# Seeds of an S4 convolution kernel without square roots: arc tangent of a turned ratio, modulus by its sine and cosine, and another prologue order

## The chip, the cores and the metric

One core of a Trainium2 chip runs the whole program. The metric is the device time of one launch in microseconds (us). Engines are called as in the profile: PE is TensorE (matmuls), DVE is VectorE, ACT is ScalarE, POOL is GpSimd, SP is SyncE, which here only issues DMAs.

## What is computed

A conditioned block. Six modulation rows come from one vector, a state space layer is applied as a long convolution, and a bilinear gated unit follows. Sizes: L = 2048 positions, D = 640 channels, N = 192 states, F = 1536.

```python
mod = (silu(c) @ w_mod).reshape(6, D)                 # sa, ca, ga, sb, cb, gb
h = layernorm(x) * (1 + ca) + sa
dt = exp(log_dt)[:, None];  A = A_re + 1j*A_im
P = exp((dt * A)[:, :, None] * arange(L))             # D x N x L
K = einsum("dn,dnl,dn->dl", C, P, dt * B).real        # one filter per channel
y = irfft(rfft(h padded) * rfft(K padded))[:L] + h * Dskip
x = x + ga * y
h = layernorm(x) * (1 + cb) + sb
x = x + gb * (((h @ w_gate) * (h @ w_up)) @ w_down)
```

The filter K is the real part of a sum of 192 terms per channel, each of which is a modulus and a phase: C·B·dt gives the start of both (the weight's modulus, and its angle), dt·A_re gives the step of the modulus' logarithm and dt·A_im the step of the phase.

## The kernel before, in words

The channels are split into five blocks `db` of 128. For each block `u_seeds(db)` (L595) works out small 128x192 tables, the seeds: the logarithm's step `rho`, the phase step `f` in turns, the weight's modulus `amp`, and the weight's angle, which becomes the integer phase `psi`. The seeds are written as steps with one letter each, and the strings `SEG0` (block 0, run in the prologue, loop at L1401) and `SEG` (blocks 1 to 4, dropped into the main loop at times from a table) say which steps run together and in what order:

- l loads; a forms rho and f; b forms x and y, the weight's real and imaginary part (L648 to L651).
- c transposes rho and f on PE (`trans`, L617 to L620, three passes each) and squares x and y on ACT; u adds the squares (L687); d and D build integer phase tables DL and DH for the block's two halves (L667 to L675).
- r and R (L681, L683) build the arguments RL and RH of the exponentials, half by half. e and E take the exponentials on ACT (tables LP, RH, RL).
- x takes the square root on ACT and |x|, and the sign of x on DVE (L693). f (L706 to L711) forms amp, and y/(|x|+modulus), with a reciprocal at L708. g is the arc tangent on ACT, whose half angle is doubled later by a scale.
- G transposes amp, h the angle; v (L736, L737) copies both out of PSUM as RL's fourth row and as psi.

From the seeds POOL builds tables (`tab_ph` L768, `tab_eq` L790, doublings at L766) and then outer products at L802: integer phases Ph, and the moduli EQ and EP, 40 "segments" in all, eight to a block. ACT turns phases into sine and cosine (`trig` L841: ab, tra or trb), DVE multiplies the two (QtA and QtB at L857 to L859, PtA at L864, PtB at L884), and PE sums over the states (kg, L899 and L914). Buffers EQ and EP are two deep, Pha and Phb too. Around these, units of the transforms (multiplications at L1022 to L1028, for example) and of the layer norm (BATCH_NORM_STATS2 at L565, the row statistics' reciprocal square root at L371 to L378) are placed at due times of a written table (`T0`), each engine working through its own instructions in the order in which the program issues them. The order strings of the buffers (`SLOT`) name the ring buffer of each use.

The modulation rows need silu(c), `sil`, which ACT forms in `mod_i`; in the prologue that stands right behind step b (P_MOD = 1). `modrow` (L451, matmul at L455) multiplies `sil` with pieces of w_mod, which `mod_l` (L442) loads into two buffers that later hold other tables, t_tw and t_ti. These matmuls are issued before the first kg matmuls, and the third piece is loaded into t_tw again only once the matmuls on the first piece have read it.

After about 530 us follows the gated unit, bound by its matmuls (L1182 and L1597); no seed work is left there. ACT's functions come in sets: an ACT_TABLE_LOAD stands before an ACTIVATE whose function isn't in the loaded set.

Of the kernel before, what the change touches and what calls it, by code (L numbers as in the profile page):

```python
# [10 lines left out]
F32 = mybir.dt.float32  # L11
# [7 lines left out]
P = 128  # L19
D = 640  # L20
# [294 lines left out]
def tile_kernel(ctx: ExitStack, tc: tile.TileContext, I, out):  # L315
# [268 lines left out]
    LP = [pk1.tile([P, 96, 8], F32, name=f"LP{i}") for i in range(3)]  # L584
    LH = pk1.tile([P, 192, 8], I32, name="LH")
    for t in LP:
        V.memset(t[:, :, 0:1], 1.0)
    RH = [pk1.tile([P, 11, 96], F32, name=f"RH{i}") for i in range(3)]
    RL = [pk1.tile([P, 4, 96], F32, name=f"RL{i}") for i in range(2)]
# [5 lines left out]
    def u_seeds(db):  # L595
# [7 lines left out]
        rho, f, amp = prm[:, 0, :], prm[:, 1, :], prm[:, 0, :]  # L603
        x, u, y, v = tb_[:, 0, :], tb_[:, 1, :], ta[:, 1, :], ta[:, 1, :]
# [3 lines left out]
        Rh, Rl, Dh, Dl, Lp = ([R[(2 * db + h) % len(R)] for h in range(2)] for R in (RH, RL, DH, DL, LP))  # L608
        g4 = lambda t: t.rearrange("p k (s r) -> p k s r", r=24)
# [7 lines left out]
        def trans(src, o):  # L617
            PE.matmul(o[:, :, 0:16], src[:, 0:128], perm[:, 0:128], start=True, stop=True)
            PE.matmul(o[0:64, :, 16:24], src[:, 128:192], perm[:, 128:192], start=True, stop=True)
            PE.matmul(o[64:128, :, 16:24], src[:, 128:192], perm[:, 192:256], start=True, stop=True)  # L620
# [32 lines left out]
        def s_c():  # L653
            ps = bank("ps").rearrange("p c (s r) -> p c s r", r=24)
            T["ps"] = ps
            trans(rho, ps[:, 0])
            trans(f, ps[:, 1])
            q = bank("q")
            act(u, x, AF.Square)
            act(q[:, 0], y, AF.Square)  # L660

        def s_d(h):
            ps, q = T["ps"], T["q"]
            sti = q[:, 1].bitcast(I32).rearrange("p (s r) -> p s r", r=24)
            free(h, "lh", "ph")
            if h == 0:
                V.tensor_copy(sti, ps[:, 1])  # L667
# [6 lines left out]
            if h:  # L674
# [3 lines left out]
        def s_r(h):  # L678
            ps = T["ps"]
            free(h, "ep", "eq", "lq")  # L680
            V.tensor_tensor(g4(Rl[h])[:, 0:3], ps[:, 0, hs[h]].unsqueeze(1).to_broadcast([P, 3, 4, 24]),  # L681
                            mults[:, 11:14].unsqueeze(2).unsqueeze(3).to_broadcast([P, 3, 4, 24]), op=OP.mult)
            V.tensor_tensor(g4(Rh[h]), ps[:, 0, hs[h]].unsqueeze(1).to_broadcast([P, 11, 4, 24]),  # L683
                            mults[:, 0:11].unsqueeze(2).unsqueeze(3).to_broadcast([P, 11, 4, 24]), op=OP.mult)

        def s_u():
            V.tensor_tensor(u, u, T["q"][:, 0], op=OP.add)  # L687
# [7 lines left out]
        def s_e(h):  # L695
            for l in range(1, 8):
                act(Lp[h][:, :, l : l + 1], Rl[h][:, 0].unsqueeze(2), AF.Exp, scale=64.0 * l)
            act(Rh[h], Rh[h], AF.Exp)
            act(Rl[h][:, 0:3], Rl[h][:, 0:3], AF.Exp)
            mark("lp", 2 * db + h)  # L700

        def s_f():
            pe = T["pe"]
            if db:
                need(1, "gg")
            V.scalar_tensor_tensor(amp, u, dt2[:, db : db + 1], pe[:, 1], op0=OP.mult, op1=OP.mult)  # L706
            V.scalar_tensor_tensor(pe[:, 0], pe[:, 0], 1e-37, u, op0=OP.max, op1=OP.add)
            V.reciprocal(pe[:, 0], pe[:, 0])  # L708
            V.scalar_tensor_tensor(y, y, 2.0, pe[:, 1], op0=OP.mult, op1=OP.mult)
            V.tensor_tensor(pe[:, 0], y, pe[:, 0], op=OP.mult)  # L710
            V.tensor_scalar(y, pe[:, 0], 1.0, -1.0, op0=OP.min, op1=OP.max)  # L711

        def s_G():
            if db:
                ps = bank("ps2")
            else:
                ps = ring(ps_tr, [P, 2, 512], "tr")[:, :, :N]
            T["ps2"] = ps.rearrange("p c (s r) -> p c s r", r=24)
            trans(amp, T["ps2"][:, 0])
            if db == 0:  # L720
                for h in range(2):
                    act(g4(Rl[h])[:, 3], T["ps2"][:, 0, hs[h]])

        def s_g():
            if db:
                s_G()
            act(y, y, AF.Arctan)

        def s_h():
            trans(y, T["ps2"][:, 1])  # L730

        def s_v():
            ps = T["ps2"]
            if db:
                for h in range(2):
                    V.tensor_copy(g4(Rl[h])[:, 3], ps[:, 0, hs[h]])  # L736
            V.tensor_scalar(psi, ps[:, 1], 4294967296.0 / math.pi, None, op0=OP.mult)  # L737
# [6 lines left out]
            for h in range(2):  # L744
# [4 lines left out]
        steps = dict(l=s_l, a=s_a, b=s_b, c=s_c, d=one(s_d, 0), D=one(s_d, 1), r=one(s_r, 0), R=one(s_r, 1), u=s_u, x=s_x,  # L749
                     e=one(s_e, 0), E=one(s_e, 1), f=s_f, G=s_G, g=s_g, h=s_h, v=s_v)  # L750
# [39 lines left out]
    def tab_eq(hf):  # L790
# [4 lines left out]
        rl = RL[hf % 2]  # L795
# [22 lines left out]
    def mk_ep(n):  # L818
        hf, s = divmod(n, 4)
        r = slice(s * 24, s * 24 + 24)  # L820
        need(1, "lp", hf)
        mark("ep", n)
        outer(EP[n % 2], LP[hf % 3][:, r], RH[hf % 3][:, 3::-1, r], 24, 4, OP.mult)

    def mk_eq(n):
# [4 lines left out]
        outer(EQ[n % 2], LQ[:, r], RH[hf % 3][:, 3:11, r], 24, 8, OP.mult)  # L830
# [566 lines left out]
    SY.dma_start(dcol, I["A_Dskip"].rearrange("(b p) -> p b", p=P))  # L1397
    exp_acc(dt, ldt)
    V.tensor_scalar(dt2, dt, 2.0, None, op0=OP.mult)
    due(-101)  # L1400
    for i, _ in enumerate(gp0):  # L1401
        due(i - 100)
        if i == P_PH:
            tab_ph(0, 1)
            mk_ph(0, 1)
        elif i == P_EP:
            mk_ep(0)
        elif i == P_MOD:
            mod_i()
    tab_eq(0)  # L1410
    tab_ph(0, 0)
    mk_ph(0, 0)
    mk_eq(0)
# [350 lines left out]
```

## Time and profile before

| what | value |
| --- | --- |
| time, median of 3 runs | 995.83 us (995.24 to 996.85) |
| the profiled execution's own time | 1000.16 us |
| its span in the trace | 998.3 us |
| granted clock of PE, mean | 0.955 |
| PE busy | 889.1 us (89%) |
| DVE busy | 770.0 us (77%) |
| ACT busy | 581.0 us (58%) |
| POOL busy | 574.7 us (58%) |

The busy shares are averages over stages of different kind. The prologue (to about 27 us) makes block 0's seeds, the main loop (to about 430 us) works through the 40 segments, and the rest is the last transforms and the gated unit. A row of the timeline is the start, the duration, the engine, the line and the operation, with what came out and went in; in square brackets stands how long the engine had been idle before and what released it. A row of a table by stretches gives the busy time of each engine with its instructions. A row of the chain gives start, duration and what the program's end was waiting for at that time.

### The profile page before, as it was taken

What the parts mean: (1) busy time and instruction counts of PE and PEld (TensorE: products, weight loads), DVE (VectorE), ACT (ScalarE), POOL (GpSimd) and SP (SyncE); (2) the same over time, 40 slices, a digit from 0 to 9 for tenths busy, and PEclk for the clock granted to TensorE, in tenths of its full rate; (3) what the DMA queues carried; (4) which work ended last, traced back from release to release, by engine and by line L of the source; (5) the groups of instructions that cost most, each with busy time, mean ns of one, the idle gap of its engine ahead of it and who ended that gap; (6) DMA issues with size and microseconds to landing.
All of it is one profiled execution on the core that took longest, in us unless ns stands there. A gap on an engine that the chain in (4) does not pass through costs nothing.

```text
span 998.3 us, 26784 instructions
## 1 busy us (share of the span) xinstructions
PE 889.1 (89%) x11190; PEld 728.2 (73%) x11190; DVE 770.0 (77%) x1391; ACT 581.0 (58%) x1055; POOL 574.7 (58%) x424
## 2 busy tenths in 40 slices
PE   4874699799889778997988999999999999999998
PEld 3653466576666466776766888879998888889998
DVE  8698568987989988795989877787576887768452
ACT  4759999987889797874574222235473422224331
POOL 4976899899869989960056667650112454442000
PEclk9867799899989989999999999999999999999999
DMA  7654665454545534559732542535635232212341
GB/s 243 239 145 155 217 237 163 159 165 135 154 131 161 171 108 149 161 152 305 221 113 59 188 169 69 184 132 159 211 133 202 96 98 80 79 53 63 96 159 53
DMA packets 141961, 148.96 MB, mean 149 GB/s; under 512 B 8976, under 2 KB 120080, under 8 KB 140432
## 3 DMA queue, kind: packets, MB, share of 16 engines
q1 hardware_dynamic: 140688, 146.33, 46.3%
q8 instruction: 88, 1.44, 0.6%
q10 hardware_dynamic: 1152, 0.92, 0.3%
q14 instruction: 33, 0.27, 0.1%
HBM read 108.36 MB, written 38.86 MB: 147 GB/s over the span
## 4 chain that ended last, share of the span: by engine, by line
PE 59%; ACT 14%; DVE 13%; issue 6%; POOL 5%; DMA 2%; DVEq 0%; SPq 0%; ACTq 0%; POOLq 0%
PE pa L1182 26%; PE pa L1597 16%; ACT tra L320 2%; ACT L320 2%; PE psfc L981 1%; ACT trb L320 1%; PE kg L899 1%; PE psfb L981 1%; PE psfa L1041 1%; PE kg L914 1%; POOL EQ L802 1%; PE psfb L1041 1%; PE psfa L981 1%; PE psfc L936 1%; POOL Pha L802 1%
## 5 line engine op out<-in xcount | busy, mean ns | idle before, releaser
L802 POOL TENSOR_TENSOR EQ<-LQ,RH 128x1536 f32<-128x1536 f32 x40 | 124.2, 3105 | 21.9 <-DVE QtB L859 21.7
L320 ACT ACTIVATE z<-pa 128x512 f32<-128x512 f32 x24 | 14.4, 599 | 166.4 <-PE pa L1182 115.4
L1146 DVE TENSOR_TENSOR wsgl<-wga,wsgh 128x640 fp32r<-128x640 f32 x72 | 68.2, 950 | 46.7 <-ACT wsgh L320 46.7
L320 ACT ACTIVATE wsgh<-wga 128x640 fp32r<-128x640 f32 x72 | 52.6, 732 | 71.2 <-PE pa L1597 39.8
L1546 POOL TENSOR_TENSOR z<-z,s 128x512 f32<-128x512 f32 x24 | 33.5, 1395 | 98.6 <-DVE s L1545 98.6
L1597 PE MATMUL pa<-wsgh,sh 128*128 128x384 f32 (+1 forms) x304 | 69.6, 310 | 0.0
L1597 PE MATMUL pa<-wsgl,sh 128*128 128x384 f32 (+1 forms) x304 | 69.3, 309 | 0.0
L1597 PE MATMUL pa<-wsgh,sl 128*128 128x384 f32 (+1 forms) x304 | 69.2, 309 | 0.0
L802 POOL TENSOR_TENSOR EP<-LP,RH 128x768 f32<-128x768 f32 x40 | 66.1, 1653 | 0.0
L1158 POOL TENSOR_TENSOR tf<-wur,wgb 128x256 f32<-128x256 f32 x24 | 19.2, 801 | 80.9 <-DVE wtl L1146 54.7
L802 POOL TENSOR_TENSOR Pha<-LH,DH 128x1536 int32<-128x1536 int32 (+1 forms) x21 | 62.5, 2974 | 3.0 <-ACT trb L320 2.6
L802 POOL TENSOR_TENSOR Phb<-LH,DH 128x1536 int32<-128x1536 int32 x20 | 62.3, 3117 | 2.9 <-ACT tra L320 2.9
L1146 DVE TENSOR_TENSOR wtl<-tf,wth 128x256 fp32r<-128x256 f32 (+1 forms) x72 | 60.0, 859 | 0.0
L914 PE MATMUL kg<-QtB,PtB 64*32 64x64 f32 x2560 | 47.9, 226 | 8.4 <-DVE QtB L858 8.4
L914 PEld LDWEIGHTS kg<-QtB,PtB 64*32 64x32 f32 x2560 | 40.9, 113 | 16.0 <-DVE QtB L858 9.5
L1544 DVE TENSOR_TENSOR s<-pa,s 128x512 f32<-128x512 f32 x24 | 16.6, 691 | 45.2 <-PE pa L1182 40.1
L1182 PE MATMUL pa<-sl,wth 128*128 128x512 f32 x144 | 45.2, 395 | 2.1 <-DVE sl L1146 2.1
L1597 PEld LDWEIGHTS pa<-wsgh,sl 128*128 128x128 f32 x304 | 46.6, 188 | 0.0
L1597 PEld LDWEIGHTS pa<-wsgl,sh 128*128 128x128 f32 x304 | 46.6, 188 | 0.0
L1597 PEld LDWEIGHTS pa<-wsgh,sh 128*128 128x128 f32 x304 | 46.5, 188 | 0.0
L1182 PE MATMUL pa<-sh,wth 128*128 128x512 f32 x144 | 45.1, 395 | 1.1 <-ACT sh L320 1.1
L1182 PE MATMUL pa<-sh,wtl 128*128 128x512 f32 x144 | 45.4, 397 | 0.0
(608 smaller groups left out, 2957.3 us busy)
## 6 DMA issues: line engine op xcount, KB each, us to landing
wga<-wdg SPq DMA_DIRECT2D x24, 640.0 KB, 4.0
wga<-B_w_gate SPq DMA_DIRECT2D x12, 640.0 KB, 5.7
wgb<-B_w_gate SPq DMA_DIRECT2D x24, 320.0 KB, 3.4
wur<-B_w_up SPq DMA_DIRECT2D x24, 320.0 KB, 4.0
xb<-x2d SPq DMA_DIRECT2D x6, 1280.0 KB, 7.4
TVb<-WD SPq DMA_DIRECT2D x22, 256.0 KB, 3.4
t_tw<-w_mod SPq DMA_DIRECT2D x3, 1600.0 KB, 7.8
t_ti<-w_mod SPq DMA_DIRECT2D x3, 1600.0 KB, 7.7
```

The source lines that it names most:

```text
L320: return S.activation(o, i, f, **kw)
L802: G.tensor_tensor(o.rearrange("p x (h l) -> p x h l", l=8), lo.unsqueeze(2).to_broadcast([P, rows, nh, 8]), hi.rearrange("p h x -> p x h") ...
L899: PE.matmul(kg[j * 32 : j * 32 + 32, dd, :], PtA[:, c, dl * 4 + j, :], QtA[:, c, dl * 4 + j, :], start=dd == 0 and c == 0, stop=False, til ...
L914: PE.matmul(kg[j * 32 : j * 32 + 32, dd, :], PtB[lo : lo + 64, c, r, :], QtB[lo : lo + 64, c, r, :], start=False, stop=dd == 7 and c == 1, ...
L981: PE.matmul(r[c][par * 64 : par * 64 + 64, i, :], t_tw[:, k0 + k, c, :], src[:, k, :], start=True, stop=True, tile_position=(0, par * 64))
L1041: PE.matmul(r[par][:, i], w, v, start=c == 0, stop=c == 1, tile_position=(lo, 0))
L1146: V.tensor_tensor(lo, v, hi, op=OP.subtract)
L1158: G.tensor_tensor(t[:, 0:2], u[:, 0:2], g[:, 0:2], op=OP.subtract)
L1182: PE.matmul(ps, w[a][:, k], x[b][:, l], start=n == 0 and m == 0, stop=n == 2 and m == len(ks) - 1)
L1544: V.tensor_tensor(S67[i], ps, S6[i], op=OP.add)
L1546: G.tensor_tensor(ZT[i], ZT[i], S67[i], op=OP.add)
L1597: PE.matmul(ACC[tb][t][c], x[:, ts], w[:, cs], start=st, stop=f == NF - 1 and n == 2 and (c == 0 or t % 2 == 1))
```

## The change

1. No square root, square or absolute value. Step x (now L700 to L704) forms a sign from x·y, sgn = ±0.5, and turns (x, y) by an eighth of a circle toward the axis, so that the ratio y/x lies within ±1; step X (L708 to L711) forms that ratio with a reciprocal. ACT takes its arc tangent, and then the sine and the cosine of the angle. The modulus is x·cos + y·sin: step m (L725) scales both products, and `trans` (L625) sums the two in PSUM while it transposes them, six passes where amp took three. Step n (L720) adds the turn of a quarter circle times sgn back to the angle.
2. For blocks 1 to 4 the exponentials of both halves are taken together (B, E): LP, RH and RL are single tiles, and one instruction takes both halves where two stood.
3. The prologue has another order. A first sine of a constant stands ahead of everything on ACT, `mod_i` (silu) moves from behind step b to behind steps m and G, where mk_ep, tab_eq and mk_eq stand as well, and tab_ph(0,0) with mk_ph(0,0) stands behind steps v and r, ahead of the exponentials' outer products.

ACT_TABLE_LOADs in the program: 24 before, 16 after.

```diff
-SEG0 = ("l", "a", "b", "c", "ud", "r", "x", "e", "f", "G", "g", "D", "h", "v", "R", "")
-SEG = ("l", "a", "b", "c", "ud", "D", "r", "R", "x", "eE", "f", "g", "h", "v")
-P_PH, P_EP, P_MOD = 3, 6, 1
+SEG0 = ("l", "a", "b", "cx", "d", "X", "f", "nh", "vr", "e", "mG", "D", "", "", "R", "")
+SEG = ("l", "a", "b", "cx", "d", "D", "X", "B", "f", "E", "nm", "G", "h", "v")
+P_PH, P_PSI, P_EP = 3, 7, 9
...
-            q = bank("q")
-            act(u, x, AF.Square)
-            act(q[:, 0], y, AF.Square)
+            bank("q")
...
-        def s_u():
-            V.tensor_tensor(u, u, T["q"][:, 0], op=OP.add)
...
         def s_x():
-            pe = bank("pe")
-            act(u, u, AF.Sqrt)
-            act(pe[:, 0], x, AF.Abs)
-            V.tensor_scalar(pe[:, 1], x, 0.0, 0.5, op0=OP.is_ge, op1=OP.subtract)
+            q = T["q"][:, 0]
+            V.tensor_tensor(q, x, y, op=OP.mult)
+            V.tensor_scalar(sgn, q, 0.0, 0.5, op0=OP.is_ge, op1=OP.subtract)
+            V.scalar_tensor_tensor(prm, tb_[:, 1::-1, :], 2.0, sgn.unsqueeze(1).to_broadcast([P, 2, N]), op0=OP.mult, op1=OP.mult)
+            V.tensor_tensor(x, x, prm[:, 0, :], op=OP.add)
+            V.tensor_tensor(y, y, prm[:, 1, :], op=OP.subtract)
+
+        def s_X():
+            q = T["q"][:, 0]
+            V.reciprocal(q, x)
+            V.tensor_scalar(q, q, 3e38, -3e38, op0=OP.min, op1=OP.max)
+            V.tensor_tensor(q, y, q, op=OP.mult)
+            V.tensor_scalar(arg, q, 1.0, -1.0, op0=OP.min, op1=OP.max)
 
         def s_f():
-            pe = T["pe"]
+            T["pe"] = pe = bank("pe")
+            act(arg, arg, AF.Arctan)
+            act(pe[:, 1], arg, AF.Sin)
+            act(pe[:, 0], arg, AF.Sin, scale=-1.0, bias=halfpi)
+
+        def s_n():
+            V.scalar_tensor_tensor(arg, sgn, 0.5 * math.pi, arg, op0=OP.mult, op1=OP.add)
+
+        def s_m():
             if db:
                 need(1, "gg")
-            V.scalar_tensor_tensor(amp, u, dt2[:, db : db + 1], pe[:, 1], op0=OP.mult, op1=OP.mult)
-            V.scalar_tensor_tensor(pe[:, 0], pe[:, 0], 1e-37, u, op0=OP.max, op1=OP.add)
-            V.reciprocal(pe[:, 0], pe[:, 0])
-            V.scalar_tensor_tensor(y, y, 2.0, pe[:, 1], op0=OP.mult, op1=OP.mult)
-            V.tensor_tensor(pe[:, 0], y, pe[:, 0], op=OP.mult)
-            V.tensor_scalar(y, pe[:, 0], 1.0, -1.0, op0=OP.min, op1=OP.max)
+            V.scalar_tensor_tensor(xy, xy, dt2[:, db : db + 1], T["pe"], op0=OP.mult, op1=OP.mult)
+
+        def s_e(*hh):
+            lp, rh, rl = (halves(R, hh) for R in (LP, RH, RL))
+            for l in range(1, 8):
+                act(lp[:, :, :, l], rl[:, :, 0], AF.Exp, scale=64.0 * l)
+            act(rh, rh, AF.Exp)
+            act(rl[:, :, 0:3], rl[:, :, 0:3], AF.Exp)
...
         def s_G():
...
-            trans(amp, T["ps2"][:, 0])
+            ps = p2()
+            trans(ps[:, 0], x, y)
...
-        def s_g():
-            if db:
-                s_G()
-            act(y, y, AF.Arctan)
...
+    act(colT[:, 0:1], halfpi, AF.Sin)
     exp_acc(dt, ldt)
-    V.tensor_scalar(dt2, dt, 2.0, None, op0=OP.mult)
+    V.tensor_scalar(dt2, dt, math.sqrt(0.5), None, op0=OP.mult)
...
+        elif i == P_PSI:
+            tab_ph(0, 0)
+            mk_ph(0, 0)
         elif i == P_EP:
+            mod_i()
             mk_ep(0)
-        elif i == P_MOD:
-            mod_i()
-    tab_eq(0)
-    tab_ph(0, 0)
-    mk_ph(0, 0)
-    mk_eq(0)
+            tab_eq(0)
+            mk_eq(0)
```

Three places show what the change does to the engines' orders. In the names, tra and trb are the PSUM buffers of sine and cosine, which also serve block 0's transposes; psfa to psfc are a ring of PSUM banks; ptb, pta and prm are the seeds' tiles in SBUF (ptb holds x and y); ct holds the permutation for the transposes; ccol is c.

ACT from its first instruction on, before: silu is the fourth ACTIVATE.

```order
L320 ACT_TABLE_LOAD
L320 ACTIVATE prm<-pta,dt 128x192
L320 ACTIVATE psfb<-ptb 128x2x192
L320 ACT_TABLE_LOAD
L320 ACTIVATE sil<-ccol 128x5
L320 ACTIVATE ptb<-ptb 128x192
L320 ACTIVATE psfa<-pta 128x192
L320 ACT_TABLE_LOAD
```

The same place after; the two rows of psfb<-pta are the sine and the cosine.

```order
L320 ACTIVATE psfb<-ptb 128x2x192
L320 ACTIVATE pta<-pta 128x192
L320 ACTIVATE psfb<-pta 128x192
L320 ACTIVATE psfb<-pta,halfpi 128x192
L320 ACT_TABLE_LOAD
L320 ACTIVATE LP<-RL 128x96 x7
L320 ACTIVATE RH<-RH 128x1056
L320 ACTIVATE RL<-RL 128x288
L320 ACTIVATE RL<-tra 128x2x96
L320 ACT_TABLE_LOAD
L320 ACTIVATE sil<-ccol 128x5
L320 ACTIVATE TVb<-psfb 1x256
```

Silu, with a table load of its own ahead of it, now stands behind the arc tangent, the exponentials and the copy of the transposed modulus.

PE from its fifth row on, after: the transposes of the angle (pta) and of x and y (ptb), and then the first modulation row. Before, three passes of amp (prm) stood there ahead of three of the angle, and the same row behind them.

```order
L625 MATMUL tra<-ct,pta 128x8x16
L625 MATMUL tra<-ct,pta 64x8x8 x2
L625 MATMUL tra<-ct,ptb 128x8x16 x2
L625 MATMUL tra<-ct,ptb 64x8x8 x4
L455 MATMUL psfb<-t_tw,sil 128x256 x5
```

The modulation row keeps its place behind the seeds' transposes, whose number grows from six to nine.

DVE in the main loop, where block 2's seeds stand between the products of two segments, before:

```order
L857 TENSOR_TENSOR QtA<-tra,EQ_143 128x32x32
L858 TENSOR_TENSOR QtA<-tra,EQ_143 128x16x32
L859 SCALAR_TENSOR_TENSOR QtA<-tra,EQ_143 128x16x32
L687 TENSOR_TENSOR ptb<-ptb,psfc 128x192
L667 CAST psfc<-psfa 128x192
```

And after:

```order
L869 TENSOR_TENSOR QtA<-tra,EQ_143 128x32x32
L870 TENSOR_TENSOR QtA<-tra,EQ_143 128x16x32
L871 SCALAR_TENSOR_TENSOR QtA<-tra,EQ_143 128x16x32
L700 TENSOR_TENSOR psfc<-ptb 128x192
L701 TENSOR_SCALAR pta<-psfc 128x192
L702 SCALAR_TENSOR_TENSOR prm<-ptb,pta 128x384
L703 TENSOR_TENSOR ptb<-ptb,prm 128x192
L704 TENSOR_TENSOR ptb<-ptb,prm 128x192
L676 CAST psfc<-psfa 128x192
```

One instruction with an operand in PSUM (psfc) gives way to five, and L700, L702, L703 and L704 read two operands from SBUF.

More of the change, by code (lines that the diff above doesn't have):

```diff
@@ L702, in s_f @@
-        def s_f():
-            pe = T["pe"]
+            for h in hh:
+                free(h, "ep", "eq", "lq")
+            w = slice(4 * hh[0], 4 * hh[-1] + 4)
+            for R, n, k in ((RL, 3, 11), (RH, 11, 0)):
+                o = halves(R, hh)[:, :, 0:n]
+                src = ps[:, 0, w].rearrange("p s r -> p (s r)").rearrange("p (h x) -> p h x", h=len(hh))
+                V.tensor_tensor(o, src.unsqueeze(2).to_broadcast([P, len(hh), n, 96]),
+                                mults[:, k : k + n].unsqueeze(1).unsqueeze(3).to_broadcast([P, len(hh), n, 96]), op=OP.mult)
@@ L734, in s_v @@
             if db:
-                for h in range(2):
-                    V.tensor_copy(g4(Rl[h])[:, 3], ps[:, 0, hs[h]])
-            V.tensor_scalar(psi, ps[:, 1], 4294967296.0 / math.pi, None, op0=OP.mult)
+                V.tensor_copy(RL[:, 0:2, 3], ps[:, 0].rearrange("p (h s) r -> p h (s r)", h=2))
+            V.tensor_scalar(psi, ps[:, 1], 2147483648.0 / math.pi, None, op0=OP.mult)
             def weighted(h):
```

74 lines of the change are left out of this document (33 added, 41 removed).

## The prediction

> **What bounds the kernel now.** I read the page's busy shares first, then the busy time by stretches.
>
> ```profile
> PE 889.1 (89%) x11190; PEld 728.2 (73%) x11190; DVE 770.0 (77%) x1391; ACT 581.0 (58%) x1055; POOL 574.7 (58%) x424
> ```
>
> ```profile
> 27.40:80.00 52.60, 36.43 (x571) 28.77 (x569) 44.14 (x95) 34.72 (x63) 42.52 (x25) 0.79 0.61 181
> 80.00:130.00 50.00, 31.77 (x644) 24.40 (x646) 35.38 (x69) 49.47 (x85) 40.63 (x27) 0.74 0.61 205
> 180.00:230.00 50.00, 45.26 (x1014) 35.06 (x1016) 43.35 (x71) 44.42 (x84) 44.70 (x29) 0.93 0.49 153
> 530.00:998.00 468.00, 458.85 (x2422) 404.78 (x2422) 328.57 (x523) 163.57 (x317) 172.64 (x158) 1.00 0.37 121
> ```
>
> The columns are the stretch, its length, and the busy time of PE, PEld, DVE, ACT and POOL. The 89% of PE come from the last stage (458.85 of 468 us), which the change doesn't touch. In the main loop three engines are close together: in 180 to 230 DVE has 43.35, ACT 44.42 and POOL 44.70 us of 50. From 80 to 130 ACT alone is full, 49.47 of 50. So a microsecond of ACT is worth one in block 1, and in blocks 2 to 4 DVE and ACT count about alike. Then I read the chain of what ended last, at the prologue:
>
> ```profile
> 17.15 0.37 ACT pta L320
> 17.56 0.79 PE tra L618 x2
> ...
> 18.77 4.57 PE psfb L455 x10
> ...
> 27.05 6.77 DMA t_tw<-w_mod
> ...
> 39.57 1.03 PE kg L899 x64
> ```
>
> The program's end hangs on the first modulation row. It starts at 18.77; once the matmuls of this piece have read t_tw, another piece of w_mod is loaded there; and behind the matmuls on that load stands the first kg at 39.57. What starts this row later moves the whole chain.
>
> **The prologue: +7.7 us.** The prices of its steps are in these rows of the timeline:
>
> ```profile
> 8.79 0.34 DVE L651 TENSOR_TENSOR pta<-pta,psfb 128x192 f32<-128x192 f32 x1
> ...
> 10.05 0.37 DVE L667 CAST psfa<-psfc 128x192 int32<-128x192 f32 x1
> ...
> 11.80 0.45 DVE L681 TENSOR_TENSOR RL<-psfc,mults 128x288 f32<-128x288 f32 x1
> 12.17 1.25 DVE L683 TENSOR_TENSOR RH<-psfc,mults 128x1056 f32<-128x1056 f32 x1
> ...
> 17.02 0.87 DVE L565 BATCH_NORM_STATS2 st<-f16a 128x6 f32<-128x320 f32 x2
> ```
>
> ```profile
> 8.03 0.21 ACT L320 ACTIVATE sil<-ccol 128x5 f32<-128x5 f32 x1
> ...
> 12.77 1.43 ACT L320 ACTIVATE LP<-RL 128x96 f32<-128x96 f32 x7
> 13.99 1.08 ACT L320 ACTIVATE RH<-RH 128x1056 f32<-128x1056 f32 x1
> ...
> 15.85 1.28 ACT L320 ACT_TABLE_LOAD   x1
> ```
>
> Before, silu was ready at 8.24, so the row waited for nothing but PE. After, silu stands behind the whole seed chain. In order: y ends at 9.13 (L651). Step x is four 128x192 operations at about 0.39 (L651's 0.34 and the gap to the next) and one of 128x384 at 0.56, 2.1. Step d is 1.75 (from 10.05 to 11.80) and 0.27 for t64, 2.0. Step X is a reciprocal of 1.40 (L708 in block 4's rows below, with its gap) and three operations at 0.39, 2.6. Arc tangent, sine and cosine are three times 0.37, as pta at 17.15: 1.1. Step n is 0.4, the angle's transpose 1.2 (from 17.56 to 18.77), psi 0.4, RL and RH 1.6 (11.80 to 13.42). Layer norm statistics come next on DVE, 1.1 (L565 and its aggregate), and m, 0.6. The exponentials run beside these and cost nothing: 2.6 us from RL on end at 22.0, before m at 22.2. The transposes of x and y have six passes each where 1.2 us had three, 2.4; the copy on ACT 0.4, the load 1.28, silu 0.2. The sum is 9.13 + 2.1 + 2.0 + 2.6 + 1.1 + 0.4 + 1.2 + 0.4 + 1.6 + 1.1 + 0.6 + 2.4 + 0.4 + 1.28 + 0.2 = 26.5, against 18.77: **+7.7**. Queued behind the waiting row on PE are five more rows and every kg; SP's reload of t_tw waits for them. The three loads fewer in the prologue lie on ACT before this point and are in the sum. If all of it were swallowed by later idle time, the term would be 0. I take it whole, since each link of the chain releases the next without slack.
>
> The load's price has two readings. The trace has 1.28 us, and the next ACTIVATE starts 0.02 us after its end (15.85 + 1.28 = 17.13, and pta starts at 17.15). The Trainium skill, page "ScalarE: Activation LUTs", section "What ACT_TABLE_LOAD costs", adds a drain of 1.38 us to each, 2.66 us in all. By it the eight loads that go would be worth 21.3 us and by the row 10.3 us; the trace disagrees with the drain, and the sum goes by the row.
>
> **Block 1: −2.4 us.** The loads on ACT from 95 to 110 us, as one group, and POOL's first operation after the place of block 1's step x:
>
> ```profile
> L320 ACT ACT_TABLE_LOAD x4 | 5.1, 1283 | 0.0
> ```
>
> ```profile
> 82.48 3.10 POOL L802 TENSOR_TENSOR EQ<-LQ,RH 128x1536 f32<-128x1536 f32 x1 [7.07 <-DVE QtB L859]
> ```
>
> Two of these loads go (2 × 1.28). The joint exponentials save 0.75: LP's seven stand 0.18 apart for 96 columns (the row at 12.77), one of 192 columns about 0.27, so seven pairs save 0.6, and the pairs of RH and RL the rest. Squares, root and absolute value less two sines are two ACTIVATEs at 0.27, 0.5. Together −3.9, all of it on a full engine. Against it stands DVE's step x of 2.1 us less 0.6 for L687 and its gap, ahead of the row statistics on which ACT's layer norm waits: +1.5. Net **−2.4**. POOL is idle for 7.07 us up to 82.48, so DVE doesn't stall there.
>
> **Blocks 2 to 4 on DVE: +1.25 us each, and stalls.**
>
> ```profile
> 356.22 0.40 DVE L706 SCALAR_TENSOR_TENSOR prm<-ptb,dt,psfc 128x192 f32<-128x192 f32 x1
> ...
> 357.06 1.37 DVE L708 RECIPROCAL psfc<-psfc 128x192 f32<-128x192 f32 x1
> ...
> 359.25 0.36 DVE L711 TENSOR_SCALAR pta<-psfc 128x192 f32<-128x192 f32 x1
> ```
>
> L706 to L711 take 3.4 us (356.22 to 359.61), and L687 and L693 0.55. The joint copies and products save 0.45. Added are x 2.1, X 2.6, n 0.4 and m 0.56, together 5.65: net +1.25. The stalls are the larger part. Two operands in SBUF cost DVE this, while POOL ran its own:
>
> ```profile
> 51.02 0.17 DVE L480 TENSOR_TENSOR mcol<-mcol 128x5 f32<-128x5 f32 x1
> 51.22 1.43 DVE L481 TENSOR_SCALAR mcol<-mcol 128x5 f32<-128x5 f32 x1
> 52.68 3.01 DVE L482 TENSOR_TENSOR mcol<-mcol 128x5 f32<-128x5 f32 x1
> ```
>
> ```profile
> 50.00 2.62 POOL L766 TENSOR_TENSOR LH<-LH,DL 128x384 int32<-128x384 int32 x2
> 52.58 3.09 POOL L802 TENSOR_TENSOR EQ<-LQ,RH 128x1536 f32<-128x1536 f32 x1
> ```
>
> L482 multiplies five columns and takes 3.01 us: it ends at 55.69, where POOL's EQ ends at 55.67. L481 ends with POOL's doubling at 52.62. L480, of the kind that takes 0.17, got through between. So such an operation waits for the end of the running POOL operation, or gets through free: 0 to 3.1 us. The seeds before had an operand in PSUM in each of these operations, and didn't wait. Where x will stand, POOL runs without a gap:
>
> ```profile
> 159.32 0.34 DVE L687 TENSOR_TENSOR ptb<-ptb,psfc 128x192 f32<-128x192 f32 x1
> ...
> 260.50 0.34 DVE L687 TENSOR_TENSOR ptb<-ptb,psfc 128x192 f32<-128x192 f32 x1
> ...
> 343.16 0.34 DVE L687 TENSOR_TENSOR ptb<-ptb,psfc 128x192 f32<-128x192 f32 x1
> ```
>
> ```profile
> 159.17 3.11 POOL L802 TENSOR_TENSOR Pha<-LH,DH 128x1536 int32<-128x1536 int32 x1
> ...
> 162.92 1.52 POOL L766 TENSOR_TENSOR LQ<-LQ,RL 128x192 f32<-128x192 f32 x2
> ...
> 258.15 3.11 POOL L802 TENSOR_TENSOR Pha<-LH,DH 128x1536 int32<-128x1536 int32 x1
> 261.22 3.10 POOL L802 TENSOR_TENSOR EQ<-LQ,RH 128x1536 f32<-128x1536 f32 x1
> ...
> 341.73 3.10 POOL L802 TENSOR_TENSOR EQ<-LQ,RH 128x1536 f32<-128x1536 f32 x1
> 344.79 1.64 POOL L802 TENSOR_TENSOR EP<-LP,RH 128x768 f32<-128x768 f32 x1
> ```
>
> L700 would wait 2.96 (159.32 to 162.28), 0.76 and 1.67 us, mean 1.8. Then L701 reads PSUM, and L702, 0.74 us behind the end of that wait, meets the next operation: 1.4, 2.3 and 0.9 us, mean 1.5. L703 and L704 follow at once, and I take them as free like L480. For n I take half of a 1.64 us EP, 0.8. Together **4.1 us a block**, an estimate within 0 and 10. Queued behind the stalled x on DVE are d and the next segment's QtA and PtA, for which PE's kg and POOL's buffers wait.
>
> No row shows a SCALAR_TENSOR_TENSOR (L702, L720) waiting like this. The Trainium skill, page "SBUF — State Buffer", section "Who interferes with whom", says that any DVE instruction with two SBUF inputs contends with a POOL instruction that reads SBUF, under an exclusive lock; it speaks against this change. By it the 4.1 stands, and if only the kinds seen to wait did so, it would be 1.8; L482's 3.01 agrees.
>
> **Blocks 2 to 4 on ACT: −2.5 us each.** One load (1.28), 0.75 and 0.5, as in block 1. In block 3, POOL's wait for psi shrinks too:
>
> ```profile
> 286.07 0.39 POOL L742 TENSOR_TENSOR DL<-ptb 128x96 int32<-128x96 int32 x1 [8.09 <-issue]
> ```
>
> ```profile
> 283.20 0.35 ACT L320 ACTIVATE pta<-pta 128x192 f32<-128x192 f32 x1
> ```
>
> The arc tangent at 283.20 came behind 6.5 us of exponentials and loads; it will stand ahead of them. Between nothing and 4.6 us of POOL's 8.09 go; I take half, −2.3.
>
> **The sum.** 7.7 − 2.4 + 3 × (1.25 + 4.1 − 2.5) − 2.3 = +11.5. The profiled execution took 1000.16 us (span 998.3), so its like would take 1011.7 us; the median of the runs is 4.3 lower, 995.83 + 11.5 = **1007** us.
>
> **The rivals.** (B) Ports don't stall DVE: the larger operations get through as L480 did. Then 12.3 go, and 995 us is left. For it speaks L480 at 0.17, while POOL's L766 ran; against it, that POOL has no gap at these places and that the two operations behind L480 waited. (C) The other side: ACT alone sets the pace of blocks 2 to 4. DVE's 1.25 + 4.1 = 5.35 us fit into its idle time (50 − 43.35 = 6.65 us in a stretch that holds one block's seeds), and only ACT's relief counts: 7.7 − 2.4 − 7.5 − 2.3 = −4.5, 991 us, faster. It decides once a block's DVE surplus stays below those 6.65 us and falls where nothing waits; against it, POOL waited 7.07 us for DVE's QtB ahead of 82.48. (D) L703 loses as well, as L482 did right behind L481: another 3.1 a block, 1017 us. (E) The late first row is swallowed by idle time further on, such as the 7.07 us ahead of 82.48: 7.7 less, 1000 us.
>
> **How the numbers follow.** Chances: forecast 0.50, B 0.14, C 0.14, D 0.14, E 0.08. A measurement of this kernel can tell about 0.2% (2 us) from no change. B straddles that bound, 0.09 within, 0.03 above and 0.02 below; the forecast's low tail adds 0.01 within; C is faster in 0.13 and within in 0.01. So faster 0.15, same 0.11, slower 0.74. The range leaves out D's upper and C's lower part: 991 to 1020 us.
>
> **What would show it.** The first modulation row should start near 26.5 and the first kg near 47; were it before 42, the prologue is wrong. L700 and L702 should last 1 to 3 us in blocks 2 to 4, ending with POOL operations, and 0.4 and 0.6 in the prologue; were they short everywhere, B holds. ACT in 80 to 130 should still be full. Should L703 be long, D holds. If DVE is long but PE's kg come no later by segment, C holds. The last stage should keep its length of 468 us; if that moved, no part of this would tell why.

## The result, and the profile after

The changed kernel takes 1040.74 us (median of 4 runs) against 995.54 us for the kernel before: the ratio is 1.0438, with a 95% interval of 1.0394 to 1.0481. It is 45 us slower, where I had forecast 11.5 us slower and a range that ended at 1020. The direction was right, and so were the prologue's term and the mechanism of the waits for POOL. A PSUM bank that is held longer was not in the sum at all, and the terms for the work of DVE and ACT were wrong.

The page of the profile after, first part, and below it the busy time by stretches (stretch, its length, then PE, PEld, DVE, ACT, POOL):

```profile
span 1041.4 us, 26793 instructions
...
PE 900.2 (86%) x11220; PEld 734.1 (70%) x11220; DVE 784.2 (75%) x1392; ACT 568.2 (55%) x1001; POOL 575.6 (55%) x424
```

```profile
80.00:130.00 50.00, 28.08 (x541) 20.15 (x544) 37.45 (x82) 40.56 (x64) 35.14 (x25) 0.73 0.55 164
...
180.00:230.00 50.00, 38.61 (x826) 29.87 (x830) 36.88 (x56) 38.32 (x65) 32.49 (x20) 0.85 0.39 120
...
280.00:330.00 50.00, 34.38 (x695) 24.68 (x695) 40.61 (x69) 34.96 (x60) 29.76 (x23) 0.86 0.45 133
...
380.00:430.00 50.00, 30.76 (x704) 22.94 (x706) 41.33 (x70) 33.22 (x55) 34.91 (x24) 0.83 0.29 86
```

The span grew by 43.1 us, and no engine's busy time by more than 14.2. In 180 to 230, which holds most of block 2's seeds, every engine is idle more than before: PE has 38.61 where it had 45.26, DVE 36.88 (43.35), ACT 38.32 (44.42) and POOL 32.49 (44.70). ACT is no longer full in 80 to 130, 40.56 of 50. When all engines lose busy time at once, they are most likely waiting for each other, and the question is where the ring of waits is closed.

To find the place I took the starts of the same 40 POOL operations (EQ at L802, now L814) in both traces and subtracted. The table gives the lag of the n-th EQ in us; the rows left out lie between their neighbours, to within 1 us.

| segment | before, start | after, lag | what lies between |
| --- | --- | --- | --- |
| 3 | 52.58 | 7.0 | the prologue |
| 8 | 121.06 | 9.3 | block 1's seeds |
| 11 | 150.19 | 11.0 | |
| 13 | 172.25 | 11.4 | block 2's seeds begin |
| 15 | 192.46 | 23.9 | |
| 21 | 253.50 | 23.8 | nothing |
| 24 | 296.66 | 31.7 | block 3's seeds |
| 29 | 341.73 | 31.7 | nothing |
| 32 | 376.41 | 43.4 | block 4's seeds |
| 39 | 436.96 | 43.4 | nothing, to the program's end |

The lag comes in steps, one at each block's seeds, and from block 2 on it is neither made nor given back between them. The last stage keeps its 468 us. Blocks 2, 3 and 4 cost 12.9, 7.9 and 11.7 us, where my sum had 2.85 each and 2.3 less in block 3.

**The prologue** went as forecast. Two rows of ACT and two of PE:

```profile
24.40 1.28 ACT L320 ACT_TABLE_LOAD   x1
25.69 0.21 ACT L320 ACTIVATE sil<-ccol 128x5 f32<-128x5 f32 x1
```

```profile
25.95 4.63 PE L455 MATMUL psfb<-t_tw,sil 128*128 128x256 f32 x10 [1.96 <-ACT sil L320]
...
47.09 1.10 PE L911 MATMUL kg<-QtA,PtAa 128*32 128x64 f32 x64
```

The row that started at 18.70 now starts at 25.95 (forecast 26.5), and the first kg at 47.09 (forecast near 47).

**Block 2** shows most of what was missing. First DVE's step x, and the POOL operations beside it:

```profile
171.83 1.65 DVE L700 TENSOR_TENSOR psfc<-ptb 128x192 f32<-128x192 f32 x1
173.51 0.36 DVE L701 TENSOR_SCALAR pta<-psfc 128x192 f32<-128x192 f32 x1
173.98 0.56 DVE L702 SCALAR_TENSOR_TENSOR prm<-ptb,pta 128x384 f32<-128x384 f32 x1
174.57 0.59 DVE L703 TENSOR_TENSOR ptb<-ptb,prm 128x192 f32<-128x192 f32 x1
175.09 1.03 DVE L704 TENSOR_TENSOR ptb<-ptb,prm 128x192 f32<-128x192 f32 x1
...
184.59 0.36 DVE L711 TENSOR_SCALAR pta<-psfc 128x192 f32<-128x192 f32 x1
189.88 1.22 DVE L869 TENSOR_TENSOR QtA<-trb,EQ 128x1024 f32<-128x1024 f32 x1 [4.94 <-ACT tra L320]
```

```profile
170.15 3.11 POOL L814 TENSOR_TENSOR Pha<-LH,DH 128x1536 int32<-128x1536 int32 x1
173.20 0.49 POOL L808 COPY LQ<-RL 128x96 f32<-128x96 f32 x1
```

L700 takes 1.65 us instead of 0.37 and ends at 173.48, just behind POOL's Pha (173.26). L703 and L704 lose 0.2 and 0.7. That is the wait for POOL that I had counted, 2.2 us here. The larger event is on PE, and then on ACT:

```profile
185.00 0.70 PE L993 MATMUL psfc<-ghb,t_tw 128*64 128x128 f32 x4 [7.58 <-DVE pta L711]
185.48 0.64 PE L993 MATMUL psfb<-ghb,t_tw 128*64 128x128 f32 x4
```

```profile
188.30 0.60 ACT L320 ACTIVATE ghb<-psfc 128x512 f32<-128x512 f32 x1 [6.32 <-PE psfc L993]
```

PE was idle for 7.58 us until DVE's L711, the last operation of step X. L993 belongs to a transform and has nothing to do with the seeds, except that it writes into psfc: the ring of PSUM banks has three members, and step X still reads x·y's bank when the transform's turn in the ring comes. In the kernel before, the same matmuls:

```profile
163.29 0.44 PE L981 MATMUL psfc<-ghb,t_tw 128*64 128x128 f32 x4 [0.19 <-DVE ptb L675]
163.56 0.39 PE L981 MATMUL psfb<-ghb,t_tw 128*64 128x128 f32 x4
```

They waited 0.19 us, for the last of the phase tables (L675). The diff shows why: the bank's last reader had been step D, and is now step X, which the order string puts behind D and which stands in DVE's queue behind the products of a segment. PE works in order, so behind L993 stand the kg matmuls; ACT's copy of L993's result stands ahead of the sines of the next segment; and DVE's QtA at 189.88 waits 4.94 us for those. The wait costs more than its length: behind it PE's granted clock is 0.50 from 185.0 to 188.6, where before it was 1.00 from 163.2 to 166.9, and the 32 matmuls of L993 take 3.6 us (185.00 to 188.61) where they took 1.9 (163.29 to 165.19). Block 3 has the same wait, 9.97 us on L711 where before it was 0.67 on L675:

```profile
297.14 1.11 PE L972 MATMUL psfc<-hfa,ct 64*64 64x512 f32 x1 [9.97 <-DVE pta L711]
```

In block 4 no wait of PE on step X stands out. There the waits for POOL show, on DVE and on POOL itself, and behind them on PE:

```profile
376.24 0.48 DVE L700 TENSOR_TENSOR psfc<-ptb 128x192 f32<-128x192 f32 x1 [0.78 <-ACT hfb L320]
...
377.22 1.42 DVE L702 SCALAR_TENSOR_TENSOR prm<-ptb,pta 128x384 f32<-128x384 f32 x1
378.68 3.14 DVE L703 TENSOR_TENSOR ptb<-ptb,prm 128x192 f32<-128x192 f32 x1
```

```profile
376.46 1.76 POOL L814 TENSOR_TENSOR EP<-LP,RH 128x768 f32<-128x768 f32 x1
378.19 3.42 POOL L814 TENSOR_TENSOR Pha<-LH,DH 128x1536 int32<-128x1536 int32 x1
```

```profile
383.67 0.44 PE L926 MATMUL kg<-QtB,PtB 64*32 64x64 f32 x8 [5.17 <-DVE QtB L870]
```

L702 ends at 378.64, after EP's end (378.22), and L703 at 381.82, after Pha's (381.61). Pha itself shows 3.42 us where it takes 3.11; it began while L702 ran. DVE's QtB stands behind step x, and PE's kg waits 5.17 us for it.

### The profile page after: what moved, and what is told of

Read it like the earlier page. It is cut to its first block, busy times and chain, and to the rows that moved or that the text cites. A ratio compares the mean times of both kernels' runs of the same rounds, so it can differ in the third digit from the quotient of the medians.

```text
span 1041.4 us, 26793 instructions
## 1 busy us (share of the span) xinstructions
PE 900.2 (86%) x11220; PEld 734.1 (70%) x11220; DVE 784.2 (75%) x1392; ACT 568.2 (55%) x1001; POOL 575.6 (55%) x424
## 5 line engine op out<-in xcount | busy, mean ns | idle before, releaser
L814 POOL TENSOR_TENSOR EQ<-LQ,RH 128x1536 f32<-128x1536 f32 x40 | 124.2, 3105 | 44.8 <-DVE QtB L871 44.6
L814 POOL TENSOR_TENSOR Pha<-LH,DH 128x1536 int32<-128x1536 int32 (+1 forms) x21 | 62.8, 2988 | 13.9 <-ACT trb L320 13.5
L814 POOL TENSOR_TENSOR Phb<-LH,DH 128x1536 int32<-128x1536 int32 x20 | 62.2, 3112 | 10.2 <-ACT tra L320 10.2
L814 POOL TENSOR_TENSOR EP<-LP,RH 128x768 f32<-128x768 f32 x40 | 66.1, 1654 | 0.0
L926 PE MATMUL kg<-QtB,PtB 64*32 64x64 f32 x2560 | 52.0, 236 | 14.9 <-DVE QtB L870 14.3
L926 PEld LDWEIGHTS kg<-QtB,PtB 64*32 64x32 f32 x2560 | 43.9, 119 | 24.5 <-DVE QtB L870 16.5
```

What stands on the lines that cost most here:

```text
L814: G.tensor_tensor(o.rearrange("p x (h l) -> p x h l", l=8), lo.unsqueeze(2).to_broadcast([P, rows, nh, 8]), hi.rearrange("p h x -> p x h") ...
L926: PE.matmul(kg[j * 32 : j * 32 + 32, dd, :], PtB[lo : lo + 64, c, r, :], QtB[lo : lo + 64, c, r, :], start=False, stop=dd == 7 and c == 1, ...
```

## The experiments

Each kernel ran beside the kernel before on the same chip, and its ratio is to those runs. From the traces I had three theories for blocks 1 to 4. A: a PSUM bank is held longer, and PE waits for it. B: DVE's operations with two operands in SBUF wait for POOL. C: the added DVE work stands where DVE is waited for, and the removed work stood where it wasn't. For the prologue: the late first modulation row goes through to the end, or is swallowed. Lags below are those of the last EQ (segment 39) in the profiled execution, against 43.4 us of the change. Each is read from one execution: at segment 4, where before_work and before_noratio have run the same instructions as the kernel before, they already lie 1.8 us ahead of it.

**ratio_early.** X right behind x:

```diff
-SEG = ("l", "a", "b", "cx", "d", "D", "X", "B", "f", "E", "nm", "G", "h", "v")
+SEG = ("l", "a", "b", "cxX", "d", "D", "", "B", "f", "E", "nm", "G", "h", "v")
```

> The changed kernel with step X (the reciprocal and the ratio) moved up to stand right behind step x in blocks 1 to 4. The work and the operands stay the same; what changes is that the PSUM bank that holds x times y is read for the last time some 10 us earlier. Theory A (the bank is held too long, and PE's next matmuls into the same bank wait for it): PE's waits of 7.6 and 10.0 us on L711 in blocks 2 and 3 shrink to about 1 us, and the time falls by 5 to 12 us from the changed kernel's 1041, to 1029 to 1036. Theory B (waits of two-operand DVE instructions for POOL) and theory C (the added DVE work itself): the same work and the same operands, so 1041 within 3 us.

Measured: 1038.53 us, ratio to the kernel before 1.0395 (1.0341 to 1.0449), lag 38.4. The expectation of theory A was missed (that of B and C, 1041 within 3 us, holds), and the trace says why:

```profile
181.19 0.70 PE L993 MATMUL psfc<-ghb,t_tw 128*64 128x128 f32 x4 [8.55 <-DVE DH L680]
```

PE still waits 8.55 us, now for L680, the last of the phase tables. The bank is needed by the phase tables too, and moving X ahead of them only made them the late reader. The experiment did not free the bank, so it told nothing against A.

**psum_operands.** The second operands of x and n from PSUM in blocks 1 to 4 (w is the bank of transposed steps):

```diff
-V.tensor_tensor(q, x, y, op=OP.mult)
+V.tensor_tensor(q, x, w[:, 0] if db else y, op=OP.mult)
...
-V.tensor_tensor(x, x, prm[:, 0, :], op=OP.add)
+V.tensor_tensor(x, x, w[:, 0] if db else prm[:, 0, :], op=OP.add)
```

and in the same way in L702, L704 and L720.

> The changed kernel with the second operand of L700, L702, L703, L704 and L720 taken from a PSUM bank in blocks 1 to 4 instead of from SBUF; the seeds of these blocks are therefore other numbers, and only the time counts. Theory B: the waits seen in the trace on L700 to L704 go (about 2.3 in block 2, 2.1 in block 3, 3.7 in block 4), and if they are the main cause their knock-on goes with them: 20 us or more off 1041. Theory A: only these 8 us go, 1031 to 1035, and PE still waits 7 to 10 us on L711 in blocks 2 and 3. Theory C: nothing or these 8 us.

Measured: 1028.95 us, ratio 1.0325 (1.0257 to 1.0394), lag 29.1, so 14.3 us less. Block 4's step x on DVE is short now:

```profile
365.69 0.36 DVE L702 TENSOR_TENSOR psfc<-ptb,psfa 128x192 f32<-128x192 f32 x1 [1.12 <-ACT hfb L320]
366.09 0.36 DVE L703 TENSOR_SCALAR pta<-psfc 128x192 f32<-128x192 f32 x1
366.36 0.55 DVE L704 SCALAR_TENSOR_TENSOR prm<-ptb,psfa 128x384 f32<-128x384 f32 x1
```

The time lies between what theory A (1031 to 1035) and theory B (20 us off) had. Theory B is real and worth more than the 8 us of waits that the rows show, but it is a third of the 43.4 us and not all: PE's wait for X is there as before, 8.45 us in block 3.

```profile
286.82 1.11 PE L974 MATMUL psfc<-hfa,ct 64*64 64x512 f32 x1 [8.45 <-DVE pta L713]
```

**before_hold.** The kernel before, with a reader of one column of that bank at X's place:

```diff
-SEG = ("l", "a", "b", "c", "ud", "D", "r", "R", "x", "eE", "f", "g", "h", "v")
+SEG = ("l", "a", "b", "c", "ud", "D", "zr", "R", "x", "eE", "f", "g", "h", "v")
...
+        def s_z():
+            V.tensor_copy(ta[:, 0, 0:1], T["q"][:, 0, 0:1])
```

> The kernel before with one added DVE instruction per block 1 to 4: a copy of a single column out of the same PSUM bank, at the place in the order at which the changed kernel has step X. It adds about 0.1 us of work and holds the bank as long as the change does. Theory A: PE waits of several us appear ahead of the matmuls into this bank, and the time rises by 5 to 15 us, to 1000 to 1011. Theories B and C: 995 to 997, since neither an operand pair nor work worth naming is added.

Measured: 1007.60 us, ratio 1.0096 (1.0061 to 1.0131), lag 9.3. Four copies of one column cost 9 us. The lag comes in block 2 (4.5) and block 3 (4.8), the blocks in which PE waited for X, and PE's waits in them are on the copy (L690):

```profile
166.45 0.53 PE L984 MATMUL psfc<-ghb,t_tw 128*64 128x128 f32 x4 [3.44 <-DVE pta L690]
...
272.22 0.89 PE L963 MATMUL psfc<-hfa,ct 64*64 64x512 f32 x1 [3.08 <-DVE pta L690]
```

This isolates theory A: no work, no operand pair, only the time of the last read.

**psum_free.** psum_operands, and x and X write to SBUF, so that the bank is free after the phase tables:

```diff
-V.tensor_tensor(q, x, w[:, 0] if db else y, op=OP.mult)
+V.tensor_tensor(prm[:, 0, :] if db else q, x, w[:, 0] if db else y, op=OP.mult)
...
+            q = prm[:, 0, :] if db else q
             V.reciprocal(q, x)
-            V.tensor_scalar(q, q, 3e38, -3e38, op0=OP.min, op1=OP.max)
-            V.tensor_tensor(q, y, q, op=OP.mult)
+            V.tensor_scalar(q, w if db else q, 3e38, -3e38, op0=OP.min, op1=OP.max)
+            V.tensor_tensor(q, y, w if db else q, op=OP.mult)
...
```

> psum_operands (second operands from PSUM, the seeds of blocks 1 to 4 other numbers) with one thing more: steps x and X write their intermediate values into a tile in SBUF instead of the PSUM bank, which is therefore free again after the phase tables, as before the change. Instructions, places and sizes stay the same. Theory A: blocks 2 and 3 each lose the 4.5 us or so that before_hold showed, and the time falls from 1029 to 1016 to 1022. Theory C (the added DVE work delays what is queued behind it, whoever holds the bank): 1026 to 1030.

Measured: 1016.64 us, ratio 1.0176 (1.0138 to 1.0214), lag 20.5, so 8.6 us less than psum_operands. PE's waits at the two places:

```profile
171.61 0.44 PE L997 MATMUL psfc<-ghb,t_tw 128*64 128x128 f32 x4 [1.81 <-DVE DH L681]
...
276.56 0.71 PE L976 MATMUL psfc<-hfa,ct 64*64 64x512 f32 x1 [3.48 <-DVE DH L681]
```

In psum_operands these were 7.46 us (put down to a DMA that landed at about the time of L713) and 8.45; 1.81 and 3.48 are left, and what is left is again on the phase tables, which stand behind step x in DVE's queue.

**before_work.** The kernel before with nine DVE instructions as x and X have them, one operand in PSUM, results unused:

```diff
-SEG = ("l", "a", "b", "c", "ud", "D", "r", "R", "x", "eE", "f", "g", "h", "v")
+SEG = ("l", "a", "b", "cw", "ud", "D", "Wr", "R", "x", "eE", "f", "g", "h", "v")
```

> The kernel before with the nine DVE instructions of steps x and X added in blocks 1 to 4 at the places of the change, on operands of which one is in PSUM, written to tiles that nobody reads afterwards; bank and everything else as before. Adds 4.7 us of DVE work a block, no POOL wait and no longer hold by a reader. Theory C: the work is exposed there, 3 to 6 us a block, 1007 to 1019. If it were hidden: 995 to 1000, and theory A would have to carry more.

Measured: 1013.25 us, ratio 1.0146 (1.0108 to 1.0184), lag 15.5: 1.5 us in block 1, then 3.3, 4.8 and 5.9. The work costs about its own length, 4.7 us, in the mean of blocks 2 to 4, although DVE was idle for 6.65 of 50 us in 180 to 230. Part of it acts through the bank, contrary to the expectation: the first five instructions stand ahead of the phase tables, which read the bank last, and in block 3 PE waits 3.37 us for these where it waited 0.67:

```profile
271.89 1.11 PE L976 MATMUL psfc<-hfa,ct 64*64 64x512 f32 x1 [3.37 <-DVE ptb L676]
```

**before_noratio.** The kernel before without L707 to L710 in blocks 1 to 4:

```diff
+if db == 0:
     V.scalar_tensor_tensor(pe[:, 0], pe[:, 0], 1e-37, u, op0=OP.max, op1=OP.add)
     V.reciprocal(pe[:, 0], pe[:, 0])
     V.scalar_tensor_tensor(y, y, 2.0, pe[:, 1], op0=OP.mult, op1=OP.mult)
     V.tensor_tensor(pe[:, 0], y, pe[:, 0], op=OP.mult)
```

> The kernel before without L707 to L710 in blocks 1 to 4 (the ratio is left out, so the angle is another number). It takes 2.6 us of DVE work a block away at the place where the change took it away too. If that work had been on the path, 3 to 10 us are gained, 986 to 993. If it ran while PE was the one waited for (theory C), the time stays within 2 us of the kernel before, and the change could save nothing by removing it.

Measured: 997.08 us, ratio 1.0002 (0.9969 to 1.0034). 2.6 us of DVE work a block are gone and no gain can be told; the interval leaves room for 3 of the 10.4 us. Block 2 of the kernel before shows the cover: L707 to L710 ran from 183.73 to 186.28, between two transform products, the second of which needed these matmuls of PE:

```profile
182.53 0.69 PE L981 MATMUL psfa<-f16b,t_tw 128*64 128x128 f32 x4 [3.58 <-DVE TVb L1027]
...
185.71 0.67 PE L981 MATMUL psfc<-f16b,t_tw 128*64 128x128 f32 x4
```

Without them DVE waits for PE instead at this place, 2.02 us here and 2.22 us in the changed kernel:

```profile
184.71 0.69 DVE L1023 TENSOR_TENSOR TVa<-psfa,ghc 128x512 f32<-128x512 f32 x1 [2.02 <-PE psfa L982]
...
210.51 0.69 DVE L1034 TENSOR_TENSOR TVa<-psfa,ghc 128x512 f32<-128x512 f32 x1 [2.22 <-PE psfa L993]
```

**late_turn.** The change with x, X and f at the place of the former square root, in a bank taken there ("o"):

```diff
-SEG = ("l", "a", "b", "cx", "d", "D", "X", "B", "f", "E", "nm", "G", "h", "v")
+SEG = ("l", "a", "b", "c", "d", "D", "r", "R", "oxXf", "E", "nm", "G", "h", "v")
```

> The changed kernel with steps x, X and f of blocks 1 to 4 moved to the place where the kernel before has its square root (behind the exponentials' arguments, r and R apart again), in a PSUM bank taken there. Operands in SBUF as in the change. Theories A and C: the bank is free early, and the DVE work stands where DVE had been waiting for PE, so blocks 2 to 4 cost 1 to 3 us each instead of 8 to 13; with the prologue's and block 1's 11 us the time is 1009 to 1016. Theory B: the POOL waits stay, 1025 or more.

Measured: 1039.65 us, ratio 1.0397 (1.0352 to 1.0441), lag 41.9. Theories A and C had 1009 to 1016 and missed; B's 1025 or more holds, but not by its reason alone. Block 2, on DVE and on PE:

```profile
193.91 1.49 DVE L702 SCALAR_TENSOR_TENSOR prm<-ptb,pta 128x384 f32<-128x384 f32 x1
195.43 3.15 DVE L703 TENSOR_TENSOR ptb<-ptb,prm 128x192 f32<-128x192 f32 x1
...
202.83 0.61 DVE L725 SCALAR_TENSOR_TENSOR ptb<-ptb,dt,psfb 128x384 f32<-128x384 f32 x1
```

```profile
203.59 1.97 PE L948 MATMUL psfb<-ct,Kta 128*64 128x128 f32 x16 [7.49 <-DVE ptb L725]
```

From x to m the chain takes 10.3 us with its waits for POOL, far more than the cover of some 4 us there, and it holds another bank, which PE wants next: 7.49 us. A and B both came along to the new place.

**silu_early.** Silu back behind step b:

```diff
+        if i == 1:
+            mod_i()
...
-            mod_i()
             mk_ep(0)
```

> The changed kernel with silu back behind step b in the prologue, at the price of one or two more table loads there. By my step on the prologue the first modulation row starts near 18 to 19 us instead of 25.95 and the whole chain comes 7 us earlier: 1033 to 1035. The rival (the late row is swallowed by later idle time): 1038 to 1041.

Measured: 1040.77 us, ratio 1.0426 (1.0380 to 1.0472), lag 41.4. My expectation was wrong here: the first row moved from 25.95 to 25.23 only.

```profile
23.44 1.86 PE L625 MATMUL tra<-ct,ptb 128*128 128x128 f32 x12 [3.50 <-DVE ptb L725]
25.23 4.41 PE L455 MATMUL psfb<-t_tw,sil 128*128 128x256 f32 x10
```

With silu out of the way, the row waits for the transposes of x and y that stand ahead of it on PE, and these for step m. A second table load, shown at the end of this document, makes m 1.3 us later than in the change (22.83 instead of 21.52). In the change the row waited 1.96 us for silu; the rest of its lateness is that of block 0's seed chain, not of silu's place. As the row hardly moved, the rival's 1038 to 1041 came true without having been tested.

**prologue_only.** The changed prologue, and blocks 1 to 4 as before (the old steps, named o_ here, for db > 0, the new for db = 0):

```diff
-SEG = ("l", "a", "b", "cx", "d", "D", "X", "B", "f", "E", "nm", "G", "h", "v")
+SEG = ("l", "a", "b", "c", "ud", "D", "r", "R", "x", "eE", "f", "g", "h", "v")
...
+        if db:
+            steps.update(c=o_c, u=o_u, x=o_x, E=one(s_e, 1), f=o_f, g=o_g, h=o_h)
```

> The prologue of the changed kernel (block 0's seeds, its order, silu late) with blocks 1 to 4 seeded as before the change. By my step on the prologue the first modulation row starts near 26 us and everything behind it 7 to 8 us later: 1002 to 1004. The rival (swallowed by idle time further on): 995 to 998.

Measured: 1009.74 us, ratio 1.0127 (1.0072 to 1.0182), lag 7.6 from segment 11 to 14 and 9.2 at the end. The time is above the 1002 to 1004 expected: the prologue's delay goes through whole, and 1.8 us more come at segment 15 that were not traced further.

**before_joint** and **savings_only.** The kernel before with joint exponentials, and with all that the change takes away in blocks 1 to 4 (the second also leaves out L707 to L710 as above):

```diff
-"x", "eE", "f", "g", "h", "v")
+"x", "E", "f", "g", "h", "v")
...
-            act(u, u, AF.Sqrt)
+            act(u, u, AF.Abs if db else AF.Sqrt)
```

> The kernel before with the exponentials of both halves of blocks 1 to 4 taken together, and nothing else of the change: nine ACTIVATEs a block fewer, about 0.75 us of ACT. My prediction counted that at its full price, 3 us in all: 992 to 993. If ACT's time is not what is waited for, the time stays within 1 us of the kernel before.

> What the change takes away in blocks 1 to 4, with nothing of what it adds: before_joint, and in blocks 1 to 4 an absolute value in place of the square root (no load of its table; four loads fewer in all) and no L707 to L710; modulus and angle of these blocks are other numbers. My prediction counted ACT's 2.5 us a block and more in block 1 at their full price: some 11 us, 985. If neither ACT nor this stretch of DVE is what the loop waits for, the time falls by less than 3 us, 993 or more, and the change had nothing to gain here.

Measured: 995.82 us, ratio 0.9984 (0.9955 to 1.0012), and 997.05 us, ratio 0.9980 (0.9950 to 1.0010). Both intervals hold 1. The savings alone are worth at most 5 us (0.5%), and none that these runs can tell. No kernel here can be told to beat the one before.

## Why the prediction was wrong, step by step

Setting the lags side by side, the 43.4 us are: prologue 9.2 (prologue_only), the rest of blocks 1 to 4, with the added DVE work, 11.3 (psum_free less prologue_only), the held bank 8.6 (psum_operands less psum_free), waits for POOL 14.3 (the change less psum_operands). The split depends on the order in which parts are taken out; alone on the kernel before, the hold costs 9.3 and the work 15.5. It is also rough: by the ratios of the timed runs the same four parts are 12.6, 4.9, 14.8 and 11.2 us.

- **Prologue, +7.7:** right, in size at the first row (25.95 where the sum had 26.5) and in the chain that carries it; 9.2 in the end. The rival E, that it is swallowed, fell.
- **Block 1, −2.4:** wrong in sign. The lag grows from 7.0 to 11.0 by segment 11; in prologue_only, with the old seeds, it grows by 1.2 there, so some 3 us are block 1's. The two loads went, but savings_only, without them, gained nothing that can be told, so ACT's time there seems not to have been worth its full price, though ACT was full; in the changed kernel it has 40.56 of 50 us in that stretch. psum_operands and psum_free have 6.9 and 7.1 at segment 11, so the loss seems to come with the SBUF operands; but step x of block 1 shows no wait itself, single traces differ by nearly 2 us, and which instruction pays was not found.
- **Waits for POOL, 4.1 a block:** the mechanism was right, the sizes only in sum. The rows show about 2.2, 2.1 and 3.7 us in blocks 2 to 4, two thirds of the estimate. L702 waited in block 4 alone, where I had it wait in all three, and L703 and L704, which I had as free, waited in blocks 2 and 4. The operands' price by psum_operands is 14.3 against my 12.3, but by the lags 4.0 of it arise in block 1, where I had none, 4.7 in block 2, none in block 3 and 5.9 in block 4: that the sums are close is in part luck. The row of L481, which I read as two operands in SBUF, is a TENSOR_SCALAR on one tile with two constants, so it was no evidence for the pair. L702 with 1.42 us in block 4 and 1.49 in late_turn shows that a SCALAR_TENSOR_TENSOR waits too, which the Trainium skill (page "SBUF — State Buffer", section "Who interferes with whom") had said and no earlier row had shown. Rival B fell.
- **DVE work, +1.25 a block:** this is the step that failed first. "L706 to L711 take 3.4 us, and L687 and L693 0.55" were taken off at full price, though the trace of before showed PE as the one waited for at that place; before_noratio gains nothing that can be told. Of the 5.65 us added, 4.7 stood elsewhere, and before_work, where they cost 15.5 us in all, shows them exposed. In psum_free the 11.3 us come in blocks 3 and 4 (some 5 us each) and at the last segment, and none in blocks 1 and 2, so how much a block pays depends on what stands beside the work. What counts is not the balance of an engine's work but the place of each piece.
- **ACT, −2.5 a block, and −2.3 in block 3:** failed. ACT's 44 of 50 us looked like the others' share, but savings_only, where I would have had some 11 us with block 1, shows at most 5 and none that can be told. In block 3 POOL's wait for psi, where I had taken off 2.3 of 8.09 us, lost only 0.45:

```profile
317.82 0.39 POOL L754 TENSOR_TENSOR DL<-ptb 128x96 int32<-128x96 int32 x1 [7.64 <-issue]
```

- **What was not in the sum:** the PSUM bank, 8.6 us; this is the step that was missing. I listed what stands behind a waiting DVE instruction, but not who else wants the buffer that it reads. The order fence showed x·y going into psfc, where L687 had read it; the last reader of that bank had to be looked for in the steps behind it.
- **Rivals C, D and E:** C had ACT as the pace and fell with the ACT term. D, L703 losing as well, happened in full once, in block 4 (3.14 us). E fell.

What stays open: why the waits for POOL cost 14.3 us when the rows show 8. I take it that a late DVE holds the bank longer too, and PE's lower granted clock behind its waits adds to it (0.50 from 383.6 to 388.0 in block 4, behind the 5.17 us), but no run separates these.

## What to carry to other kernels

For every buffer of a ring that an edit touches, look up its last reader before and after, and who has the next turn in the ring: four copies of one column, placed late, cost this kernel 1%. Take work off at its price only where the engine was the one waited for, and add it at its price wherever the neighbours wait; two equal pieces at different places are not a balance of zero. When every engine's busy time falls in a stretch, subtract the starts of one repeated operation in the two traces, and the steps of the lag name the places.

## What the runs showed of the hardware

A POOL operation that starts while DVE works on two operands in SBUF takes longer itself: block 4's Pha shows 3.42 us and EP 1.76, where others of their shape in the same trace take 3.11 and 1.64. PE's granted clock fell to half behind long waits, in the kernel before too: it was 0.50 from 182.5 to 186.5 there, behind a wait of 3.58 us, and 0.50 from 297.1 to 302.0 in the changed kernel, behind 9.97 us. The length of the wait alone doesn't fix the moment: in savings_only the same matmuls, again behind 3.58 us, had 0.83 from 182.3 to 184.3 and 0.50 from 184.3 on. Which table set an arc tangent gets depends on what ran before it. In the changed kernel, where the first sine stands ahead, one set serves arc tangent, sine and cosine:

```profile
15.80 0.36 ACT L320 ACTIVATE pta<-pta 128x192 f32<-128x192 f32 x1 [9.11 <-DVE pta L711]
16.19 0.33 ACT L320 ACTIVATE psfb<-pta 128x192 f32<-128x192 f32 x1
```

In silu_early, with silu in between, the set loaded for the arc tangent has no sine, and a second load stands between the two:

```profile
15.82 0.36 ACT L320 ACTIVATE pta<-pta 128x192 f32<-128x192 f32 x1 [6.30 <-DVE pta L711]
16.20 1.28 ACT L320 ACT_TABLE_LOAD   x1
17.50 0.33 ACT L320 ACTIVATE psfb<-pta 128x192 f32<-128x192 f32 x1
```
